# A two-layer kernel in a new order: loads held for the turns of q, and in four batches the normalised product with tokens on partitions

## The chip, the cores and the metric

The kernel runs on one NeuronCore of a Trainium2 chip. The metric is the device time of one execution in microseconds (us), as the median of several runs. The core has a matrix engine (TensorE, "PE" in the profile), VectorE ("DVE"), ScalarE ("ACT"), GpSimd ("POOL") and SyncE ("SP"). Each has one queue of instructions that it works off in order. Transfers run on 16 DMA engines. In this kernel SP issues the stores and the DMA transposes, and POOL issues the loads that also convert float32 to bfloat16.

## What is computed

There are 8 batches of 576 tokens with 8 heads of 64. The first layer is linear attention with a normalisation, the second a channel mix of RWKV's kind:

```
kv  = einsum('bhsd,bhse->bhde', k, v)
u   = einsum('bhsd,bhde->bhse', q, kv)
x   = u / sqrt(mean(u*u, -1) + 1e-6) * g_norm          # heads side by side: [B, S, 512]
xk  = mu_k*x + (1-mu_k)*x_prev ;  xr = mu_r*x + (1-mu_r)*x_prev     # x_prev: the token before
kk  = maximum(xk @ w_k, 0)                             # 512 -> 1024
out = sigmoid(xr @ w_r) * (kk*kk @ w_v)                # 1024 -> 512
```

q, k, v and the output are float32 in HBM.

## The kernel before

The whole program is one list of words, `ORDER`. A loop at the end takes word after word and calls the function of that name, so the list fixes the order of instructions on every engine. A word is a step, its arguments, the PSUM banks that it takes (`=25`), and a `'` where VectorE does the step and not ScalarE. Nothing moves at run time: an engine that waits for one instruction holds all those behind it.

The steps of one batch, with the lines under which the profile knows them:

- `ld.0.b`, `ld.1.b`, `ld.2.b` load k, v and q (POOL; L193 for k and v, L205 and L207 for q's two parts: `in_q`, 512 tokens, and `in_qr`, the other 64). Each of k, v and q has two buffers, so that a load of batch b waits until the batch two before is done with its buffer. Batches 0 and 1 are loaded and worked in pieces by words of their own (`lf`, `kc`, `qc`, `uc`), among matmuls on zeros that bridge waits (`wm`, L246).
- `kv.b` makes kv (PE, L328, 72 matmuls on 64x64 tiles); `kvo` takes it out of PSUM.
- `qd.b.0` turns `in_q` into `qT` by a DMA transpose of 16 blocks (SP, L344); `qd.b.1` turns the small part into `qTr`, 4 blocks (SP, L346).
- `u.b.part` makes u with features on partitions: parts 0 and 1 are 8 matmuls of 256 columns each on 64x64 tiles (PE, L361), part 2 is the small part (L354).
- `sq` squares u (ACT, L372); `ms` makes the mean over a head by a matmul with a matrix of 1/64 (PE, L376; 512 columns in parts 0 and 1); `rs` is the inverse root (ACT, L381); `mu` multiplies u, g and the root into `xT` (DVE, L400).
- `d`, `sc`, `add` make xk and xr (L428, L437/L439, L448). `which` is 0 for xk and 1 for xr.
- `K.b.f.h` is xk @ w_k in 16 pieces of 4 matmuls of 288 columns (PE, L493), `Ko` the maximum with 0 (DVE L457, ACT L455), `ks` the square (DVE L463, ACT L461).
- `R.b.t` is xr @ w_r, 4 matmuls of 512 columns (PE, L513), `S` the sigmoid (ACT, L518); `V.b.t.part` is kk*kk @ w_v, twice 4 matmuls of 512 columns (PE, L523; the last tile in halves, L531); `fin` multiplies (DVE, L538); `st` stores (SP, L555).
- `tab` loads a table of activation functions (ACT, L585).

Steps of several batches stand among each other: `kv.6`, say, stands among the K steps of batch 3.

Of the kernel before, what the change touches and what calls it, by code (L numbers as in the profile page):

```python
# [30 lines left out]
    sc.0.1.2' Kf.0.2.3.256 Kf.6.0.4.256=3 Kf.7.0.4.256=1 Kfo.7.256 Kf.2.3.4.256 Kf.5.0.4.256=4 Kf.0.3.4.256
    Kfo.0.256 Kf.1.2.3.256 Kf.1.3.4.256 sc.0.1.1' add.0.1.0 wm.3=6 qc.1.0.2.0.576=67 qco.1.1.0.576 add.0.1.1
    R.0.2=1 R.0.1=5 R.0.0=7 lf.1.1.2.4.0.576 lw.2.0.0.4.0.4 sc.0.0.2.0.256' Kfo.1.256' sc.0.0.3.0.256' S.0.2
    S.0.1 sc.0.0.1.0.256' add.0.0.0.0.256 qco.1.0.0.576' R.0.3=0 S.0.3 add.0.0.1.0.256 Kfo.2.256' S.0.0
    Kfo.5.256' ksp.0.4.256.576' Kfo.6.256' ksp.4.8.256.576' Kl.0.256=1 lw.2.1.4.8.0.4 ld.2.2 qd.2.0 qd.2.1
    Klo.0.256 kc.1.0.2=65 kco.1.0' tab.0.1 qc.1.2.4.0.576=24 uc.1.0=0 kc.1.2.4=37 kco.1.3 sq.1.0 Kl.1.256=1
    qco.1.2.0.576' kco.1.2' uc.1.4=6 sq.1.4 kco.1.1' qco.1.3.0.576' uc.1.1=2 sq.1.1 uc.1.2=3 Klo.1.256'
    ksp.0.4.0.256' ms.1.0=5 rs.1.0 mu.1.0 Kl.3.256=7 sq.1.2 ms.1.4=4 rs.1.4 mu.1.4 ms.1.1=1 rs.1.1 Klo.3.256'
    Kl.2.256=5 Klo.2.256 ksp.4.8.0.256' ms.1.2=4 uc.1.3=0 sq.1.3 uc.1.5=6 sq.1.5 V.0.2.0=1 rs.1.2 mu.1.1
    ms.1.3=7 rs.1.3 V.0.2.1 ms.1.5=5 rs.1.5 tab.1.1 mu.1.2 V.0.0.0=4 V.0.0.1 mu.1.3 V.0.3.0=2 V.0.3.1 V.0.1.0=7  # L40
    mu.1.5 wrap.1 dc.1.0.2.0.576 sc.1.0.0 dc.1.2.4.0.576 sc.1.0.2 sc.1.0.3' sc.1.0.1' add.1.0.0 add.1.0.1
    sc.1.1.0 sc.1.1.1 V.0.1.1 ld.0.2 ld.1.2 sc.1.1.3 sc.1.1.2' add.1.1.0 add.1.1.1 fin.0.3 K.1.6.0=3 K.1.1.0=5
    Ko.1.1.0 fin.0.2 ld.2.3 K.1.6.1=0 Ko.1.6.0' R.1.8=6 Ko.1.6.1 S.1.8 R.1.4=5 kv.2=02 kvo.2.0 qd.3.1 kvo.2.1
    kvo.2.2' K.1.0.0=1 R.1.7=6 K.1.0.1=3 R.1.6=0 fin.0.1 kvo.2.3 S.1.4 Ko.1.0.0' u.2.1=25 Ko.1.0.1' R.1.5=7
    K.1.5.0=1 fin.0.0 st.0.0 K.1.4.0=3 Ko.1.4.0' S.1.7 S.1.6 sq.2.3 zl K.1.1.1=6 Ko.1.1.1' ks.1.1' Ko.1.5.0'
    K.1.2.0=4 Ko.1.2.0' S.1.5 sq.2.2 ms.2.2=0 tab.0.2 ms.2.3=7 rs.2.3 mu.2.3 K.1.3.0=3 Ko.1.3.0 K.1.7.0=6
    K.1.3.1=1 Ko.1.3.1' rs.2.2 mu.2.2 u.2.2=7 sq.2.4 u.2.0=43 sq.2.1 sq.2.0 ld.0.3 ld.1.3 kv.3=50 ld.2.4 qd.4.1
    Ko.1.7.0' kvo.3.0 ks.1.0' K.1.2.1=1 ks.1.3' Ko.1.2.1 ks.1.2' kvo.3.1 kvo.3.3' K.1.7.1=2 Ko.1.7.1 ks.1.7'
    ms.2.0=6 rs.2.0 mu.2.0 ms.2.1=5 rs.2.1 kvo.3.2 K.1.5.1=1 V.1.4.0=0 K.1.4.1=2 ks.1.6 Ko.1.5.1 ms.2.4=6 rs.2.4
    mu.2.1 d.2.0 d.2.4 d.2.1 V.1.7.0=5 V.1.8.0=4 Ko.1.4.1 ks.1.4' d.2.3 mu.2.4 d.2.2 sc.2.1.0' ks.1.5 tab.1.2  # L50
    V.1.6.0=3 V.1.7.1 V.1.8.1 st.0.3 V.1.4.1 sc.2.0.0 sc.2.0.3 sc.2.0.1' V.1.6.1 qd.3.0 sc.2.1.3' add.2.0.0
    sc.2.0.2' add.2.0.1 sc.2.1.1 add.2.1.0 K.2.5.0=1 sc.2.1.2' K.2.5.1=6 add.2.1.1 K.2.2.1=2 Ko.2.5.0' Ko.2.5.1
    fin.1.4 K.2.2.0=7 Ko.2.2.0' Ko.2.2.1 fin.1.7 ks.2.5' R.2.2=6 S.2.2 fin.1.8 ld.0.4 R.2.3=1 R.2.1=2 S.2.1
    S.2.3 ks.2.2' R.2.0=0 ld.1.4 K.2.3.0=7 Ko.2.3.0' st.0.2 st.1.4 S.2.0 u.3.0=56 sq.3.1 sq.3.0 u.3.2=4 sq.3.4
    K.2.3.1=2 fin.1.6 st.1.6 Ko.2.3.1' K.2.0.0=1 Ko.2.0.0' ks.2.3' ms.3.1=0 K.2.6.0=7 Ko.2.6.0' K.2.4.0=3
    Ko.2.4.0' tab.0.3 K.2.0.1=2 rs.3.1 mu.3.1 ms.3.0=1 ms.3.4=7 K.2.1.0=3 rs.3.4 Ko.2.0.1 ks.2.0' rs.3.0
    K.2.4.1=0 Ko.2.4.1 K.2.1.1=7 K.2.6.1=2 u.3.1=61 Ko.2.1.0' Ko.2.1.1 ks.2.1 kv.4=03 V.2.1.0=7 mu.3.0 sq.3.3
    ms.3.3=5 mu.3.4 sq.3.2 ms.3.2=4 Ko.2.6.1' ks.2.6' rs.3.3 mu.3.3 kvo.4.0 rs.3.2 st.1.7 mu.3.2 V.2.0.0=2 d.3.0
    d.3.4 d.3.1 d.3.2 sc.3.0.0' kvo.4.1 kvo.4.2 tab.1.3 K.2.7.1=5 V.1.5.0=0 K.2.7.0=4 Ko.2.7.0 Ko.2.7.1 V.1.5.1
    V.2.2.0=1 kvo.4.3 ks.2.4 V.2.3.0=3 sc.3.0.1 sc.3.0.3 sc.3.0.2' ks.2.7' V.2.3.1 sc.3.1.0' sc.3.1.1' add.3.1.0  # L60
    ld.2.5 V.2.1.1 V.2.2.1 add.3.0.0 add.3.0.1 K.3.0.0=6 Ko.3.0.0 K.3.0.1=4 K.3.5.0=5 K.3.2.0=6 st.0.1 st.1.8
    qd.4.0 Ko.3.5.0 sc.3.1.3' fin.2.2 sc.3.1.2' K.3.4.0=1 add.3.1.1 R.3.7=5 Ko.3.0.1' ks.3.0' fin.1.5 fin.2.1
    K.3.5.1=4 qd.5.0 fin.2.3 Ko.3.5.1' R.3.8=0 R.3.4=7 S.3.7 st.1.5 qd.5.1 Ko.3.4.0 u.4.1=51 K.3.3.0=3 Ko.3.3.0'
    sq.4.3 S.3.8 sq.4.2 R.3.6=4 S.3.6 R.3.5=3 st.2.2 st.2.3 Ko.3.2.0' K.3.2.1=0 Ko.3.2.1' ks.3.2' K.3.3.1=6
    Ko.3.3.1' V.2.0.1 fin.2.0 S.3.4 S.3.5 K.3.7.0=4 ms.4.3=7 K.3.1.0=3 tab.0.4 rs.4.3 Ko.3.1.0' K.3.1.1=0
    Ko.3.1.1 ms.4.2=6 rs.4.2 ks.3.3 K.3.7.1=2 Ko.3.7.0' ld.0.5 ld.1.5 Ko.3.7.1' kv.5=73 mu.4.2 kvo.5.0' ld.2.6
    kvo.5.1 mu.4.3 u.4.0=40 sq.4.0 ld.0.6 kvo.5.3 ld.1.6 kv.6=62 ld.2.7 ld.0.7 kvo.5.2' sq.4.1 u.4.2=5 sq.4.4
    kvo.6.0' kvo.6.1' ks.3.7' K.3.6.0=3 Ko.3.6.0 K.3.6.1=7 ms.4.1=1 Ko.3.6.1 K.3.4.1=6 ms.4.4=2 ms.4.0=3 ks.3.5'
    ks.3.1' V.3.8.0=7 rs.4.1 kvo.6.3' mu.4.1 rs.4.0 mu.4.0 d.4.0 d.4.1 V.3.7.0=1 d.4.3 Ko.3.4.1 ks.3.4 ks.3.6
    V.3.6.0=3 V.3.8.1 V.3.6.1 rs.4.4 tab.1.4 qd.6.0 mu.4.4 d.4.4 d.4.2 sc.4.1.0 sc.4.1.1' sc.4.1.3 sc.4.1.2  # L70
    fin.3.8 V.3.7.1 add.4.1.0 sc.4.0.0' st.2.1 add.4.1.1 V.3.5.0=0 V.3.5.1 fin.3.6 u.5.0=64 fin.3.7 fin.3.5
    sc.4.0.1 add.4.0.0 st.3.7 st.3.8 u.5.1=25 sq.5.3 sq.5.2 sc.4.0.3' sq.5.1 R.4.3=7 S.4.3 sc.4.0.2' add.4.0.1
    R.4.0=3 S.4.0 R.4.1=1 S.4.1 R.4.2=0 S.4.2 K.4.0.0=7 V.3.4.0=3 ms.5.2=1 Ko.4.0.0 ms.5.3=0 K.4.2.0=7 Ko.4.2.0'
    tab.0.5 rs.5.2 mu.5.2 V.3.4.1 ms.5.1=7 K.4.3.0=1 rs.5.3 K.4.1.0=0 sq.5.0 K.4.0.1=2 mu.5.3 ms.5.0=5 fin.3.4
    rs.5.1 Ko.4.3.0 mu.5.1 Ko.4.1.0' K.4.1.1=7 rs.5.0 mu.5.0 d.5.0 K.4.2.1=1 Ko.4.2.1 Ko.4.0.1 ld.1.7 u.5.2=3
    sq.5.4 kv.7=54 ks.4.2 K.4.5.0=0 Ko.4.5.0 ms.5.4=1 rs.5.4 K.4.3.1=2 Ko.4.3.1 qd.7.1 K.4.4.0=6 st.2.0
    K.4.6.1=0 K.4.6.0=1 ks.4.0' Ko.4.4.0 Ko.4.1.1' ks.4.1 qd.6.1 K.4.7.1=7 d.5.4 mu.5.4 d.5.1 d.5.2 kvo.6.2'
    sc.5.0.0' ks.4.3' Ko.4.6.0' sc.5.1.0' sc.5.0.3 sc.5.0.1' sc.5.0.2 add.5.0.0 add.5.0.1 K.4.4.1=2 kvo.7.0
    V.4.0.0=3 K.4.5.1=6 Ko.4.4.1 K.4.7.0=1 V.4.1.0=5 Ko.4.6.1 Ko.4.5.1' K.5.2.0=2 K.5.6.0=0 ks.4.6 Ko.4.7.0'
    Ko.4.7.1 ks.4.5' kvo.7.1' ks.4.4 ks.4.7' K.5.7.0=7 qd.7.0 Ko.5.6.0' sc.5.1.1' K.5.6.1=6 sc.5.1.3' Ko.5.2.0'  # L80
# [29 lines left out]
def kernel(  # L110
# [536 lines left out]
```

## Time and profile before

| | before |
|---|---|
| median of 3 runs | 210.25 us (209.4 to 211.29) |
| the profiled execution: time, span on the core | 211.27 us, 209.5 us |
| busy: PE, DVE, ACT | 193.4, 147.7, 140.4 us |
| K matmuls (L493) x448 | 64.0 us |
| V matmuls (L523) x280 | 65.4 us |
| R matmuls (L513) x144 | 34.0 us |
| HBM read, written | 33.56 MB, 9.44 MB |
| mean granted clock of PE | 0.976 |

The profile is that of one execution, whose time is beside its span; the span goes from the first instruction to the last and is a little shorter. "PEclk" is the share of full speed that PE's clock was granted. "DMA share" in a table of stretches is busy time of the 16 DMA engines over the stretch; it goes over 1 where packets overlap on an engine.

### The profile page before, as it was taken

The page shows a single profiled execution, that of the slowest core. Times are in us where ns is not written, and L with a number is a line of the kernel's source. Part 1 is how long each engine was busy: PE and PEld are TensorE (multiplying, and loading weights), DVE is VectorE, ACT ScalarE, POOL GpSimd, SP SyncE. Part 2 cuts the span into 40 slices and gives each one's busy share as a digit, 9 for nine tenths or more (in the row PEclk, how much of TensorE's full clock was granted, in tenths as well). Part 3 has the DMA queues.
Part 4 walks back from the last instruction along what each step waited for, and adds up shares of the span by engine and source line. Part 5 has one row for each costly group of instructions (what it writes and reads, how often), then busy time and mean ns, then how long its engine had stood idle before and what let it go on. Part 6 is the DMA issues. An engine that isn't in the chain of part 4 may idle for free.

```text
span 209.5 us, 4772 instructions
## 1 busy us (share of the span) xinstructions
PE 193.4 (92%) x1925; PEld 111.9 (53%) x1925; DVE 147.7 (70%) x331; ACT 140.4 (67%) x263; POOL 31.4 (15%) x49
## 2 busy tenths in 40 slices
PE   7699999995999999999549999999999999999992
PEld 2344565462765576465335457666554576755541
DVE  2159998963699787994617949985499799756242
ACT  2258779953897599638708899926997896625630
POOL 8664242000500500052400000000000000000000
PEclk9889999999999999999958999999999999999999
DMA  6999999999999799999999950732002100024425
GB/s 221 183 195 204 208 206 199 207 179 183 226 203 214 126 189 264 212 106 198 240 159 156 214 179 5 137 126 100 0 3 100 52 0 3 0 79 173 153 63 188
DMA packets 43018, 30.66 MB, mean 146 GB/s; under 512 B 19308, under 2 KB 38004, under 8 KB 42996
## 3 DMA queue, kind: packets, MB, share of 16 engines
q0 software_dynamic: 22672, 16.19, 52.5%
q1 hardware_dynamic: 20164, 14.03, 27.8%
q8 instruction: 15, 0.25, 0.5%
q10 hardware_dynamic: 160, 0.13, 0.2%
q14 instruction: 7, 0.06, 0.1%
HBM read 33.56 MB, written 9.44 MB: 205 GB/s over the span
## 4 chain that ended last, share of the span: by engine, by line
PE 60%; DMA 35%; POOL 1%; issue 1%; DVE 0%; POOLq 0%
PE ps_km L493 22%; PE ps_v L523 22%; DMA qT<-in_q 12%; PE ps_r L513 10%; DMA in_q<-in_q_dram 9%; DMA in_v<-in_v_dram 7%; DMA wk_sb<-in_moe_w_k_dram 4%; DMA q<-in_q_dram 3%; PE ps_ms L376 2%; PE ps_kv L328 1%; PE ps_u L361 1%; PE ps_v L531 1%; PE ps_u L354 1%; POOL in_k L193 0%; POOL wk_sb L214 0%
## 5 line engine op out<-in xcount | busy, mean ns | idle before, releaser
L523 PE MATMUL ps_v<-wv_sb,sqk 128*128 128x512 bf16 x280 | 65.4, 379 | 0.0
L493 PE MATMUL ps_km<-xk,wk_sb 128*128 128x288 bf16 x448 | 64.0, 289 | 0.0
L493 PEld LDWEIGHTS <-wk_sb 128*128 128x128 bf16 x448 | 43.7, 99 | 18.5 <-issue 0.6
L523 PEld LDWEIGHTS <-sqk 128*128 128x128 bf16 x280 | 27.0, 98 | 28.8 <-issue 0.4
L457 DVE TENSOR_SCALAR rt<-ps_km 128x288 bf16<-128x288 f32 (+2 forms) x64 | 28.8, 462 | 19.2 <-PE ps_km L493 18.7
L455 ACT ACTIVATE rt<-ps_km 128x288 bf16<-128x288 f32 (+2 forms) x60 | 23.8, 419 | 21.3 <-PE ps_km L493 21.0
L513 PE MATMUL ps_r<-wr_sb,xr 128*128 128x512 bf16 x144 | 34.0, 379 | 0.0
L538 DVE TENSOR_TENSOR out_sb<-ps_v,sig 128x512 f32<-128x512 f32 (+1 forms) x37 | 24.1, 671 | 11.8 <-PE ps_v L523 6.4
L372 ACT ACTIVATE sq<-ps_u 128x512 bf16<-128x512 f32 (+4 forms) x43 | 21.2, 527 | 15.8 <-PE ps_u L354 5.2
L400 DVE SCALAR_TENSOR_TENSOR xT<-ps_u,cols,rs 128x512 bf16<-128x512 f32 (+4 forms) x43 | 27.3, 659 | 4.2 <-ACT rs L381 4.0
L518 ACT ACTIVATE sig<-ps_r 128x512 bf16<-128x512 f32 x36 | 20.6, 600 | 13.5 <-PE ps_r L513 13.2
L381 ACT ACTIVATE rs<-ps_ms,eps 128x512 f32<-128x512 f32 (+4 forms) x43 | 25.7, 620 | 3.2 <-PE ps_ms L376 3.1
L513 PEld LDWEIGHTS <-xr 128*128 128x128 bf16 x144 | 13.8, 98 | 14.9 <-issue 0.4
L463 DVE TENSOR_TENSOR sqk<-rt 128x576 bf16<-128x576 bf16 (+2 forms) x40 | 18.6, 482 | 2.6 <-ACT rt L455 2.1
L585 ACT ACT_TABLE_LOAD x15 | 19.2, 1283 | 0.3
L437 ACT ACTIVATE m<-dx,cols 128x576 bf16<-128x576 bf16 (+2 forms) x25 | 17.6, 747 | 1.4 <-DVE dx L428 0.8
L461 ACT ACTIVATE sqk<-rt 128x576 bf16<-128x576 bf16 x20 | 13.4, 680 | 1.2 <-DVE rt L457 1.1
L376 PE MATMUL ps_ms<-sq,means 128*128 128x512 bf16 (+4 forms) x43 | 13.5, 349 | 0.6 <-ACT sq L372 0.4
L439 DVE TENSOR_SCALAR m<-dx,cols 128x576 bf16<-128x576 bf16 (+2 forms) x41 | 13.7, 362 | 0.2
L205 POOL DMA_DIRECT2D in_q<-in_q_dram x6 | 5.3, 891 | 49.5 <-DMA qT<-in_q 48.3
L448 DVE TENSOR_TENSOR xr<-m,xT 128x1152 bf16<-128x1152 bf16 x16 | 11.9, 754 | 0.6 <-ACT m L437 0.3
L448 DVE TENSOR_TENSOR xk<-m,xT 128x1152 bf16<-128x1152 bf16 (+2 forms) x17 | 11.6, 699 | 0.7 <-ACT m L437 0.3
(66 smaller groups left out, 131.5 us busy)
## 6 DMA issues: line engine op xcount, KB each, us to landing
out_dram<-out_sb SPq DMA_DIRECT2D x23, 256.0 KB, 2.9
in_k<-in_k_dram POOLq DMA_DIRECT2D x7, 576.0 KB, 15.2
in_v<-in_v_dram POOLq DMA_DIRECT2D x6, 576.0 KB, 16.2
in_q<-in_q_dram POOLq DMA_DIRECT2D x6, 512.0 KB, 12.9
out_dram<-out_sb SPq DMA_DIRECT2D x24, 128.0 KB, 6.8
wk_sb<-in_moe_w_k_dram POOLq DMA_DIRECT2D x4, 256.0 KB, 8.8
wv_sb<-in_moe_w_v_dram POOLq DMA_DIRECT2D x2, 512.0 KB, 16.7
sqk<-in_k_dram SPq DMA_DIRECT2D x1, 576.0 KB, 3.7
```

Source lines behind the costliest of these rows:

```text
L372: ACT.activation(out=sq[:, :ps.shape[1]], in_=ps, func=AF.Square)
L381: ACT.activation(out=rs[:, :ps.shape[1]], in_=ps, func=AF.Abs_reciprocal_sqrt, bias=eps)
L400: DVE.scalar_tensor_tensor(out=dst, in0=ps, scalar=g_sb, in1=rs, op0=ALU.mult, op1=ALU.mult)
L448: DVE.tensor_add(out=blended(a, which)[:, hs, c0:c1], in0=at[a]["m", which][:, hs, c0:c1], in1=xT[a % 2][:, hs, P + c0:P + c1])
L455: eng.activation(out=dst, in_=ps, func=AF.Relu)
L457: eng.tensor_scalar(out=dst, in0=ps, scalar1=0.0, scalar2=None, op0=ALU.max)
L493: nc.tensor.matmul(ps, wk_sb[:, cc, 128 * fc:128 * fc + 128], at[b]["xk"][:, cc, SH * h:SH * h + SH], start=(cc == 0), stop=(cc == NHP - 1))
L513: nc.tensor.matmul(ps, xr[:, cc, 128 * t:128 * t + 128], wr_sb[:, cc, :], start=(cc == 0), stop=(cc == NHP - 1))
L518: ACT.activation(out=sig[b, t], in_=give(("r", b, t)), func=AF.Sigmoid)
L523: nc.tensor.matmul(ps, sqk[:, fc, 128 * t:128 * t + 128], wv_sb[:, fc, :], start=(fc == 0), stop=(fc == NFC - 1))
L538: DVE.tensor_mul(out=o, in0=give(("v",) + key), in1=sig[b, t][:, c])
L585: "tab": lambda eng, n, b: ACT.preload_act_table_set(("abs_reciprocal_sqrt_and_small", "sigmoid_and_others")[n]),
```

## The change

**The order.** Every step stands at a new place. All 8 batches are still computed, with the same tiles for K, R and V.

**Loads and q's turns.** A new word `gt.b` is a copy of one column from `qTr` on POOL. POOL can't go on to its next load before the small turn of q of batch b has landed. It stands behind the loads of batch 2 (`gt.2`), behind those of batch 3 (`gt.3`), and, for batches 4, 5 and 6, behind the last load of all. In batch 2 the small turn now goes ahead of the large one, as it did in batch 3. In these lines the loads that followed one another on POOL are:

```
before: q2 k2 v2 q3 k3 v3 q4 k4 v4 q5 k5 v5 q6 k6 v6 q7 k7 v7
after:  q2 k2 v2 gt.2 q3 v3 k3 gt.3 v4 k4 q4 q5 v6 v5 k6 q6 k5 v7 q7 k7 gt.4 gt.5 gt.6
```

**The last four batches.** In batches 4 to 7 the parts 0 and 1 of `u` are made with tokens on partitions and heads and features along the row: `ut`, 16 matmuls of 64 columns each with a stationary piece of 64 x 128 of `qT`. `sqt` squares (ACT), `rdt` sums 64 neighbours (DVE), `rst` is the inverse root on 128x16 (ACT), `mut` multiplies (DVE) into a tile `y`, which has 3 buffers, `yd` turns `y` into `xT` by a DMA transpose of 4 blocks (SP), and `gs` multiplies by g (DVE). The mean by matmul (`ms`), `rs` and `mu` are left for the small part alone in these batches.

**Counts of the two programs** where they differ most: PE matmuls of `ms` on 512 columns 28 and 12; `u` on 256 columns 96 and 32; `ut` 0 and 128; matmuls on zeros 31 and 19. DVE: `mu` on 512 columns in batches 2 to 7 24 and 8; `rdt` 0 and 16; `mut` 0 and 16; `gs` 0 and 8; `Ko` on 288 columns 57 and 52; `sc` 37 and 32; `ks` 36 and 31. ACT: `rs` on 512 columns 28 and 12; `rst` 0 and 8; `Ko` 55 and 60; `sc` 23 and 28; `ks` 20 and 25. SP: 16 more DMA transposes.

```
+    gates = const.tile([128, B], BF16, name="gates")
...
+    def gate(a):
+        POOL.tensor_copy(out=gates[:, a:a + 1], in_=at[a]["qTr"][:, 0, 0:1])
...
+    def u_t(a, tp):
+        ps = [take(("t", a, 2 * tp + r), [128, H, HD], FP32, "ps_u") for r in range(2)]
+        for h in range(H):
+            for r in range(2):
+                nc.tensor.matmul(ps[r][:, h, :], at[a]["qT"][half(r), 2 * h + tp, :], kv_on(a, h // 2, h % 2, r), start=True, stop=True)
+
+    def square_t(a, t):
+        sq = at[a]["sqt", t] = work.tile([128, 512], BF16, tag="sq", name="sq", bufs=SQ_BUFS)
+        ACT.activation(out=sq, in_=held["t", a, t].rearrange("p h d -> p (h d)"), func=AF.Square)
+
+    def sum_t(a, t):
+        ss = mine(a, "ss", [128, 4, H], FP32)
+        DVE.tensor_reduce(out=ss[:, t, :], in_=at[a]["sqt", t].rearrange("p (h d) -> p h d", h=H), op=ALU.add, axis=AX.X)
+
+    def rsqrt_t(a, tp):
+        ACT.activation(out=mine(a, "rst", [128, 4, H], FP32)[:, 2 * tp:2 * tp + 2, :], in_=at[a]["ss"][:, 2 * tp:2 * tp + 2, :],
+                       func=AF.Abs_reciprocal_sqrt, scale=1.0 / HD, bias=eps)
+
+    def mult_t(a, t):
+        y = at[a]["y", t] = work.tile([128, 512], BF16, tag="y", name="y", bufs=SQ_BUFS)
+        DVE.tensor_mul(out=y.rearrange("p (h d) -> p h d", h=H), in0=give(("t", a, t)),
+                       in1=at[a]["rst"][:, t, :].unsqueeze(2).to_broadcast([128, H, HD]))
+
+    def y_turn(a, t):
+        c = place(a)[0] + 256 * (t % 2) + 128 * (t // 2)
+        nc.sync.dma_start_transpose(out=xT[a % 2][:, :, c:c + 128], in_=at[a]["y", t])
+
+    def gain(a, r):
+        x = xT[a % 2][:, :, place(a)[0] + 256 * r:place(a)[0] + 256 * r + 256]
+        DVE.tensor_scalar(out=x, in0=x, scalar1=g_sb, scalar2=None, op0=ALU.mult)
```

Two pieces of the new `ORDER` that the prediction speaks of, the first around the first `ut`, the second around `kv.5`:

```
ms.3.3=3 ld.1.5 ld.0.6 rs.3.3 V.1.6.0=5 zl mu.3.3 V.1.6.1 qd.4.1 st.0.1 K.2.6.0=1 u.3.2=2
fin.1.6 kvo.4.2 ut.4.0=03 ks.2.0 st.1.4 sq.3.4 ms.3.4=7 ks.2.5' mu.3.2 d.3.0 ld.2.6 ks.2.3 V.2.0.0=5
...
st.1.7 S.3.8 sqt.4.1 st.2.0 sc.3.0.3' R.3.4=2 fin.2.2 S.3.4 S.3.6 sqt.4.0 qd.5.0 ...
rst.4.0 K.3.2.0=2 Ko.3.2.0' K.3.1.0=7 Ko.3.1.0 ut.4.1=56 sqt.4.2 sqt.4.3 u.4.2=4 sq.4.4 kv.5=12 kvo.5.0
kvo.5.1 mut.4.1 K.3.7.0=7 Ko.3.7.0 yd.4.1 mut.4.0 yd.4.0 rdt.4.2 rdt.4.3 K.3.3.1=3 K.3.0.1=0 Ko.3.0.1
K.3.1.1=1 Ko.3.1.1 rst.4.1 mut.4.2 ms.4.4=2 mut.4.3 rs.4.4 st.2.2 ...
```

In the order before, `kv.5` and `kv.6` stand at:

```
Ko.3.1.1 ks.3.3 K.3.7.1=2 Ko.3.7.0' ld.0.5 ld.1.5 Ko.3.7.1' kv.5=73 mu.4.2 kvo.5.0' ld.2.6
kvo.5.1 mu.4.3 u.4.0=40 sq.4.0 ld.0.6 kvo.5.3 ld.1.6 kv.6=62 ...
```

## The prediction

> **What bounds the kernel now.** I read the page first: PE is busy 92% of the span, so time goes by PE's work and by the places where PE stands still.
>
> ```profile
> PE 193.4 (92%) x1925; PEld 111.9 (53%) x1925; DVE 147.7 (70%) x331; ACT 140.4 (67%) x263; POOL 31.4 (15%) x49
> ```
>
> The waits of PE name those places. After the start there are two, both for a DMA: the first u of batch 2 for its turned q, and kv of batch 6 for v.
>
> ```profile
> PE ps_kv L328 <- DMA in_v<-in_v_dram: 5.4, 1, 5.4
> PE ps_u L361 <- DMA qT<-in_q: 2.6, 1, 2.6
> ```
>
> The chain of waits shows how they come about: a turn of q lasts 14.1 us in one place; the next q's load is held by another turn, and v6 queues behind that load on POOL.
>
> ```profile
> 37.39 14.10 DMA qT<-in_q
> ...
> 80.43 10.48 DMA qT<-in_q
> ...
> 93.75 13.87 DMA in_v<-in_v_dram
> 107.61 0.14 issue
> 107.75 1.18 PE ps_kv L328 x55
> ...
> 109.14 2.04 PE ps_km L493 x8
> ```
>
> A turn's price depends on the loads beside it, as the rows of the tile qT show (issue to landing: shortest, median, longest). The shortest ran when the loads were over. The waits of POOL show the other side: loads held for turns.
>
> ```profile
> DMA to landing us min/median/max: 4.3/5.6/14.1
> ...
> POOL in_q L205 <- DMA qT<-in_q: 48.3, 3, 18.3
> ```
>
> In the table of stretches (PE, PEld, DVE, ACT, POOL busy, then clock, DMA share, GB/s) the wait for v6 also halves the clock. The stretch of 115 to 190 us shows PE full without a gap and DVE at 80%, ACT at 74%.
>
> ```profile
> 50.00:55.00 5.00, 3.47 (x30) 2.29 (x31) 1.03 (x4) 2.63 (x4) 1.95 (x3) 1.00 1.22 200
> 70.00:75.00 5.00, 5.00 (x44) 2.89 (x42) 3.88 (x9) 3.51 (x7) 3.08 (x4) 1.00 0.76 111
> 90.00:95.00 5.00, 5.00 (x39) 2.81 (x37) 3.79 (x8) 1.32 (x4) 3.56 (x5) 1.00 0.72 115
> 105.00:110.00 5.00, 2.25 (x84) 1.88 (x85) 0.82 (x4) 0.38 (x1) 0.00 (x0) 0.50 1.43 157
> 115.00:190.00 75.00, 75.00 (x582) 44.44 (x581) 60.07 (x131) 55.77 (x103) 0.00 (x0) 1.00 0.28 77
> ```
>
> **PE's work.** Rates come from the dense pieces of the chain: 4 K matmuls 0.49 us, 4 V or R 0.86, one 512-column mean 0.216, 16 matmuls of u (two parts) 0.56 to 0.68, one kv 0.61. Batches 4 to 7 lose 8 parts of u, 8 x 0.3 = 2.4, and 16 means, 16 x 0.216 = 3.5: -5.9. They gain 8 `ut` of 16 loads and 16 matmuls. No row has a 64x128 load before a 64-column matmul. From below: the small part of u, 8 in 0.12, 0.015 each, gives 8 x 0.24 = 1.9. From above: the weight load's row, 98 ns, one after another, 8 x 1.57 = 12.5. The nearest is kv, 72 pairs of load and matmul in 0.61: four tiles at a time, so 34 ns for a pair with 64 columns to load. Twice the columns and two tiles at a time (the two halves of qT) make about 54 ns for a load, half of it each: 0.43 per `ut`, 3.4 in all. Net -2.5 (bounds -4.0 and +6.6). Of the 12 fewer matmuls on zeros, 9 stood in the first 19 us, where PE waits for data; they are worth nothing. Three stood in dense work at 23.3 us: 3 x 0.216 = -0.65.
>
> The Trainium skill, page "TensorE: Matmul & The Clock Gate", section "LDWEIGHTS (loading the stationary operand)", puts a load at columns / 1.2 ns, 107 ns for 128, and has loads overlap only across row groups; by that a `ut` would be 0.85 and the net about +1. The kv row is faster than that rule: 53 ns for 64 columns would not fit into 34.
>
> **The two old waits.** The order of loads and the gates take away their causes: v and k of batch 4 no longer stand behind q, v6 stands ahead of q6, and the small turn of q2 goes first, with nothing but k2 and v2 beside it. I take off 2.6 and 5.35, and 2.0 for the half clock (8 K matmuls took 2.04 and not 0.98; the rest of kv, u and the mean some 0.9). Sum -9.9.
>
> **The new waits for DMA.** Where are they? I count PE's work up to a step by the rates above (matmuls on zeros left out) and set it against the clock. Before, the first u of batch 2 stands behind 32.3 us of work and was reached at 49.0: 16.7 later. POOL's loads up to v2 are the same transfers in the same order, and the start is paced by them, so I keep 16.7 (give or take 1.5 for the other order of the start). After, without waits, u of batch 2 is due at 52.7, kv.3 at 57.5, u.3 at 67.8, `ut.4.0` at 79.5, kv.5 at 92.1, kv.6 at 98.7.
>
> Against that the transfers. q2 lands at 37.4 and v2 near 44, as before. The small turn (2.3 us at the fastest, 10.0 at the slowest) opens `gt.2` near 43; qT of batch 2 lands near 48, in time for 52.7. q3 lands near 50 (a load issued on an idle queue took 6.6 to 8.3), k3 near 57: kv.3 just in time. `gt.3` opens near 55; then v4, k4, q4 land near 61, 65, 69. SP issues the large turn of batch 3 behind six stores, near 56: 66 to 71, so u.3 waits 0 to 3. The turn of batch 4 starts at 69 to 70 with q5, v6, v5 and k6 under way and no gate before these: 10.5 to 14.1 us, so 80 to 84, against 79.5. The wait here is about 4 us. PE works in order, so everything shifts with it.
>
> kv.5 needs k5, the ninth load behind k3. Before, the nine loads behind v3 (landed 56.7) ended at 107.6, 51 us, with two breaks at the shares of 0.76 and 0.72, some 5 us. Without breaks that is 46 us from 57: 103. By the faster rates between (2.8 to 3.5 us for a k or v, 3.1 to 5 for a q) I come to 97. I take 100, 8 us behind 92.1; the 4 of the turn are part of it. Then kv.6 and the rest have their data. Bounds: 0, if loads keep their best pace and the turn ends early; 14, if k5 lands at 103 and a turn of q5 behind it costs 3 more. Value 8.
>
> The 16 turns of y have 4 blocks like the small q turn: 2.3 us free, up to 10.0 beside loads. SP issues the first two right behind qT of batch 5, whose issue alone took up to 6.9 us, near 99. y has three buffers, so the fourth `mut` of batch 4 holds DVE until the first turn has landed, and behind it wait the `Ko` that free PE's banks. PE has 3 to 4 us of matmuls until a bank is missing: I take +1 (0 to 4). The later turns run after the loads, with 20 us between `ut` and K to hide them.
>
> **VectorE.** In batches 4 to 7 it loses 16 `mu` (0.746): -11.9. It gains 16 sums, 16 `mut` and 8 `gs`. `mut` is like the final product, 512 columns from PSUM, 0.685; `gs` on 1024 bf16 lies between 0.364 (576 columns) and 0.692 (a subtraction of 1024), I take 0.45. No reduction stands in the trace: 0.417 (bf16 subtraction on 512) and 0.746 are the bounds, 0.685 my value. Together 22.0 + 3.6 = 25.6, less 11.9, less 6.3 for five `Ko`, `sc` and `ks` each that go to ScalarE: +7.4. Over the 75 us of that stretch 60.1 becomes 67.5 of about 72.5: 93%. ScalarE loses 16 `rs` (11.0), gains 8 `rst` (0.3, near the 0.374 of its 128-column form) and 9.3 of moved work: +0.7. Both still fit under PE's work, at nothing; if that cover were gone, DVE's 7.4 would count in full.
>
> The Trainium skill, page "VectorE: DVE Perf Modes", section "The perf-mode tier table", has a reduction at one element per cycle whatever the type and its rules call it the slowest operation of this engine. No run here shows it so far; at 0.417 the sum for DVE would be +3.1 and not +7.4.
>
> **The end.** Before, the last product is half a tile (0.42) and the store 64 KB; now a whole tile (0.685) and 256 KB: +0.4.
>
> **Sum** on the profiled execution: -2.5 - 0.65 - 9.9 + 8 + 1 + 0.4 = -3.7. The span goes from 209.5 to 205.8, its time from 211.27 to 207.6. That execution is 1.0 above the median, so the median goes to 206.5.
>
> **The rivals.**
> 1. *The gates do all that they are for.* POOL's loads end early enough and qT of batch 4 lands before 79.5: the 9 us of new waits go, 197.5. For it: POOL issues as soon as it can, and both breaks of the share are loads that come too late. Against it: no gate stands before the loads beside the turn of batch 4.
> 2. *VectorE becomes the bound in the last four batches.* At 93% there are 5 us to spare in the 75. It decides from there on: when the pairs of a sum and a `mut` take 0.3 us more than I have (16 x 0.3 = 5), or when the hand-overs between ACT and DVE (square, sum, root, product) and the turns of y hold DVE's queue for as long. At 12 us lost, 0.75 for each of 16 tiles, PE waits 7 us more: 213.5. For it: the work between K of batch 6 and K of batch 7 asks DVE for some 10 us beside 10.7 of PE. Against it: before, DVE ran through such stretches (60 to 65 us, 4.89 of 5) without a wait of PE.
> 3. *Weight loads bound `ut`.* At 98 ns, two at a time, a `ut` takes 0.78: +2.8, 209.3, no change. The rule of columns / 1.2 named above is this case. Against it: the kv row.
>
> **Chances.** Forecast 0.45, rival 1 0.18, rival 2 0.27, rival 3 0.10. A measurement of this kernel can tell about 1% from no change, so faster means below 208.1, slower above 212.4. The forecast's own range (203 to 210) is faster in 0.37 and the same in 0.08; rival 1 is faster; rival 2 is slower in 0.21 and the same in 0.05; rival 3 is the same in 0.04, faster in 0.03, slower in 0.03. Faster 0.59, same 0.17, slower 0.24. The range is 199.5 to 213.5: it takes in most of rival 1 and 2 and the bounds of the new waits; `ut` at its upper bound (+9) is left out.
>
> **What would show it.** PE's waits: right if none stands at u of batch 2 and kv.6, and some 4 to 8 us in all at `ut.4.0` or kv.5 for DMA; wrong if there is none (rival 1), or if PE waits for DVE in batches 4 to 7 (rival 2). The `ut` row: 0.43 each. The reduction's row: near 0.685. The page's DVE total: near 152. Of the whole the forecast is wrong if the median is above 208.

## The result, and the profile after

The changed kernel takes 217.1 us (median of 4 runs, 215.3 to 217.5) against 210.7 (209.4 to 211.3). The ratio is 1.030, with an interval of 1.022 to 1.037: slower, where the prediction said 206.5. Of some kernels a few executions took over 1.5% longer than the fastest: ratios leave these out where enough others are left, medians hold them, so the two can differ a little.

The profiled execution took 216.82 us with a span of 215.1. The busy line of its page, in the order of the one shown of before:

```profile
PE 191.9 (89%) x1961; PEld 111.5 (52%) x1961; DVE 153.2 (71%) x334; ACT 141.9 (66%) x276; POOL 32.7 (15%) x54
```

PE's busy time fell by 1.5 us while the span grew by 5.6, so PE stands still for longer. The waits of PE after (engine, line, what it waited for, sum, times, longest):

```profile
PE ps_u L375 <- DMA qT<-in_q: 7.9, 1, 7.9
PE ps_km L531 <- DVE y L391: 3.2, 1, 3.2
PE ps_kv L330 <- DMA in_k<-in_k_dram: 2.4, 1, 2.4
...
PE ps_v L561 <- DVE kv L243: 0.9, 1, 0.9
```

The two old waits (u of batch 2, kv of batch 6) are gone. There are four new ones: `kv.3` for k3, the first `ut` of batch 4 for its turned q, and two where PE waits for VectorE, which itself is held. The chain of waits after shows by what:

```profile
38.44 6.32 DMA qTr<-in_qr
44.76 0.05 issue
44.81 0.19 POOL gates L351
...
47.35 11.01 DMA in_k<-in_k_dram
...
58.40 0.78 PE ps_kv L330 x72
...
74.33 16.20 DMA qT<-in_q
90.53 0.05 issue
90.58 0.61 PE ps_u L375 x16
...
108.06 0.70 DVE y L391
...
109.87 8.66 DMA xT<-y
118.53 0.03 issue
118.55 0.48 DVE xT L400
```

`gt.2` opens at 44.8 and only then q3, v3 and k3 are issued; k3 lands at 58.4. q of batch 4 lands at 74.3 and its turn takes 16.2 us, up to 90.5, while PE stood at `ut.4.0` from 82.65. In batch 4 the product `y` (L391) and the step by g (L400) hang on the turns of y. The rows of the tile y, with who waited (us, times) and then issue to landing (shortest, median, longest):

```profile
  DVE y L391: 6.1, 3
  PE ps_km L531: 3.2, 1
  DVE xT L400: 1.9, 1
...
DMA to landing us min/median/max: 2.4/3.2/8.7
```

The longest of these are the turns issued from 105.6 on, the last of them landed at 118.5, beside the loads of v7 and q7 and a store; the shortest come later, with no load beside them. The rows of POOL and PE in that stretch (start, us, what, in brackets the idle time before it) show v7 issued right behind the end of `kv.5`, and PE standing still:

```profile
105.58 0.74 POOL L195 DMA_DIRECT2D in_v<-in_v_dram  x1 [12.17 <-PE ps_kv L330]
...
114.12 1.12 PE L531 MATMUL ps_km<-xk,wk_sb 128*128 128x288 bf16 x4 [3.20 <-DVE y L391]
```

Over the same stretches as before, and some more, the table (PE, PEld, DVE, ACT, POOL, clock, DMA share, GB/s) shows where the clock goes:

```profile
55.00:60.00 5.00, 2.57 (x88) 1.38 (x87) 4.29 (x8) 2.33 (x5) 1.43 (x3) 0.94 1.13 262
...
85.00:90.00 5.00, 0.00 (x0) 0.00 (x0) 0.00 (x0) 0.00 (x0) 0.00 (x0) 0.67 1.30 126
90.00:95.00 5.00, 4.42 (x29) 2.08 (x30) 2.75 (x8) 2.59 (x5) 2.32 (x3) 0.64 1.02 239
...
110.00:115.00 5.00, 1.80 (x12) 0.99 (x9) 1.59 (x4) 1.48 (x4) 0.00 (x0) 0.90 1.33 185
115.00:120.00 5.00, 4.07 (x113) 2.69 (x113) 3.08 (x10) 3.48 (x8) 0.00 (x0) 0.75 1.25 230
120.00:205.00 85.00, 85.00 (x660) 50.54 (x659) 72.64 (x154) 59.01 (x112) 2.42 (x5) 1.00 0.41 97
```

At 85 to 90 us every engine is idle and only transfers run. From 120 us on PE has no gap. All that was lost was lost before.

**The account of 5.6 us of span.** Gaps of PE over 0.1 us after 20 us of the span: 8.1 before, 14.8 after. Matmul time at half clock after 20 us: 3.5 before (104.5 to 111.3), and after 3.4 (59.4 to 62.8), 3.0 (86.7 to 93.6) and 3.3 (114.0 to 117.5), 9.7 in all; half of it is lost, 1.8 and 4.9. The tail behind the last matmul grew by 0.2. So +6.7 + 3.1 + 0.2 = +10.0. The span grew by 5.6, so PE's work and the start together gave 4.4; this is the remainder, not a measurement. By place: `kv.3` 2.4 + 1.7, `ut.4.0` 7.9 + 1.5, the hold by the y turns 3.2 + 0.9 + 1.7.

The rows of the new operations (busy us, mean ns of one):

```profile
L391 DVE TENSOR_TENSOR y<-ps_u,rst 128x512 bf16<-128x512 f32 x16 | 10.7, 687 | 8.1 <-DMA xT<-y 6.1 <-ACT rst L386 1.9
L383 DVE TENSOR_REDUCE ss<-sq 128x8 f32<-128x512 bf16 x16 | 10.4, 678 | 1.1 <-ACT sq L379 1.1
L400 DVE TENSOR_SCALAR xT<-xT,cols 128x1024 bf16<-128x1024 bf16 x8 | 3.8, 479 | 1.9 <-DMA xT<-y 1.9
L375 PE MATMUL ps_u<-kv,qT 64*128 64x64 bf16 x128 | 3.6, 208 | 7.9 <-DMA qT<-in_q 7.9
L375 PEld LDWEIGHTS <-qT 64*128 64x128 bf16 x128 | 2.8, 106 | 8.9 <-DMA qT<-in_q 8.0 <-issue 0.7
```

### The profile page after: what moved, and what is told of

Same layout as the page of the kernel before. It is cut to its first block, busy times and chain, and to the rows that moved or that the text cites. A ratio compares the mean times of both kernels' runs of the same rounds, so it can differ in the third digit from the quotient of the medians.

```text
span 215.1 us, 4891 instructions
## 1 busy us (share of the span) xinstructions
PE 191.9 (89%) x1961; PEld 111.5 (52%) x1961; DVE 153.2 (71%) x334; ACT 141.9 (66%) x276; POOL 32.7 (15%) x54
## 4 chain that ended last, share of the span: by engine, by line
PE 58%; DMA 36%; POOL 2%; DVE 1%; issue 1%; SPq 0%; ACT 0%; POOLq 0%
PE ps_v L561 25%; PE ps_km L531 18%; PE ps_r L551 11%; DMA in_qr<-in_q_dram 8%; DMA qT<-in_q 8%; DMA wr_sb<-in_moe_w_r_dram 5%; DMA in_k<-in_k_dram 5%; DMA xT<-y 4%; DMA q<-in_q_dram 3%; DMA qTr<-in_qr 3%; PE ps_kv L330 1%; PE ps_u L375 1%; PE ps_v L569 1%; POOL wk_sb L216 1%; PE ps_ms L414 1%
## 5 line engine op out<-in xcount | busy, mean ns | idle before, releaser
L531 PE MATMUL ps_km<-xk,wk_sb 128*128 128x288 bf16 x448 | 59.0, 287 | 3.2 <-DVE y L391 3.2
L576 DVE TENSOR_TENSOR out_sb<-ps_v,sig 128x512 f32<-128x512 f32 (+1 forms) x37 | 24.0, 671 | 10.4 <-issue 4.1
L495 DVE TENSOR_SCALAR rt<-ps_km 128x288 bf16<-128x288 f32 (+2 forms) x57 | 25.0, 465 | 8.8 <-PE ps_km L531 8.4
L438 DVE SCALAR_TENSOR_TENSOR xT<-ps_u,cols,rs 128x512 bf16<-128x512 f32 (+4 forms) x27 | 16.0, 608 | 14.7 <-ACT rs L419 14.4
L475 ACT ACTIVATE m<-dx,cols 128x576 bf16<-128x576 bf16 (+1 forms) x29 | 20.9, 759 | 8.2 <-DVE dx L463 3.5
L419 ACT ACTIVATE rs<-ps_ms,eps 128x512 f32<-128x512 f32 (+4 forms) x27 | 15.2, 581 | 13.1 <-PE ps_ms L414 12.8
L499 ACT ACTIVATE sqk<-rt 128x576 bf16<-128x576 bf16 x25 | 16.6, 680 | 3.5 <-DVE rt L495 3.1
L501 DVE TENSOR_TENSOR sqk<-rt 128x576 bf16<-128x576 bf16 (+2 forms) x35 | 16.5, 487 | 0.9 <-ACT rt L493 0.6
L391 DVE TENSOR_TENSOR y<-ps_u,rst 128x512 bf16<-128x512 f32 x16 | 10.7, 687 | 8.1 <-DMA xT<-y 6.1
L410 ACT ACTIVATE sq<-ps_u 128x512 bf16<-128x512 f32 (+4 forms) x27 | 12.6, 487 | 5.2 <-PE ps_u L359 4.2
L383 DVE TENSOR_REDUCE ss<-sq 128x8 f32<-128x512 bf16 x16 | 10.4, 678 | 1.1 <-ACT sq L379 1.1
```

The lines of the kernel that those rows point to most:

```text
L475: eng.activation(out=out_, in_=in_, func=AF.Copy, scale=mu)
L495: eng.tensor_scalar(out=dst, in0=ps, scalar1=0.0, scalar2=None, op0=ALU.max)
L499: eng.activation(out=dst, in_=src, func=AF.Square)
L501: eng.tensor_mul(out=dst, in0=src, in1=src)
L531: nc.tensor.matmul(ps, wk_sb[:, cc, 128 * fc:128 * fc + 128], at[b]["xk"][:, cc, SH * h:SH * h + SH], start=(cc == 0), stop=(cc == NHP - 1))
L576: DVE.tensor_mul(out=o, in0=give(("v",) + key), in1=sig[b, t][:, c])
```

## The experiments

The explanations go by letters. A (runs 1 to 4): the gates hold the loads longer than the faster turns give back, and y's three buffers hold VectorE. B (runs 2 and 4): the new form asks too much of VectorE. C (from run 5 on): what the DMA engines have to move in the first 105 us is given; the new order asks for its data some 5 to 8 us too early, and an edit of order moves the wait and does not remove it. D, the rival of C in run 5: a turn is slow because it shares the engines with loads, and nothing else counts. Words of `ORDER` are shown as the edit where that is all. Lines of the experiments are a few lower than those of the changed kernel, since their list is wrapped otherwise (`ut` is L370 and `u` L361, in place of L375 and L366). "Before" ran beside each group: 210.5 to 211.0.

**1. No gates.**

```
- every gt.2 gt.3 gt.4 gt.5 gt.6
```

> The changed kernel without any gate (the words gt.2 to gt.6 are left out), else the same. Theory A, the gates cost more than they give: they kept POOL from loading for 16.4 and 10 us while the DMA engines ran out of loads, so q3 landed at 51.3 and q4 at 74.3. Without them q3 lands near 48.5, k3 near 56.7 (wait of kv.3 2.4 to under 1), q4 near 68, the large turn of batch 4 ends near 82 to 84 and not at 90.5, so that its wait falls from 7.9 to 0 to 4 us, with less half clock: 208 to 212 us. Rival, the gates protect the turns: the first u of batch 2 waits for its turn again (2 to 5 us), the turn of batch 4 still takes 16 us or more, and the time stays at 216 us or rises.

Measured 219.2 (215.0 to 221.0), ratio 1.027 (1.016 to 1.038). The waits of PE:

```profile
PE ps_u L361 <- DMA qT<-in_q: 7.3, 1, 7.3
...
PE ps_kv L325 <- DMA in_k<-in_k_dram: 5.1, 1, 5.1
```

The wait at `ut.4.0` is gone, and 7.3 us stand at u of batch 2 and 5.1 at `kv.5`. A falls: the gates move the wait.

**2. Six buffers for y; 3. both edits.**

```
-        y = ... tag="y", name="y", bufs=SQ_BUFS)
+        y = ... tag="y", name="y", bufs=6)
```

> The changed kernel with 6 buffers for y and not 3. Theory A, the turns of y cost only through y's buffers: the wait of the product (L391) for DMA xT<-y, 6.1 us, goes, and with it PE's 3.2 and 0.9 us around 111 to 119 us and the half clock behind them (1.7): 211 to 213.5 us. Rival B, the new form of u asks too much of VectorE: the same delay shows as waits of PE for other DVE work, 216 us or more.

> Both edits together: no gates, 6 buffers for y. Theory A: the two gains add, 203 to 208 us, faster than the kernel before; PE waits 0 to 4 us after its start. Rival (gates protect the turns, or VectorE is the bound): 212 us or more.

Measured 218.8, ratio 1.039 (1.032 to 1.046), and 219.4, ratio 1.032 (1.025 to 1.040). With six buffers `mut` no longer waits, but the step by g does, and PE behind it:

```profile
DVE xT L395 <- DMA xT<-y: 6.9, 1, 6.9
...
PE ps_v L556 <- DVE kv L238: 6.1, 1, 6.1
```

So the buffers alone are not the cause; VectorE waits for the late turns all the same. Without gates as well, most of it stands at `kv.5` (10.2 for k5).

**4. The new order with the old form of u** in batches 4 to 7 (`sq`, `ms`, `rs`, `mu` in the places of the new steps, no y, six buffers for the squares).

> The new order with its gates, but batches 4 to 7 make u in the old form (features on partitions, mean by matmul, root on 512 columns, one product into xT; no turn of y, no g step); 6 buffers for squares and roots. This leaves the order's DMA waits and takes away the new form. Theory A, the form costs only through y's buffers: PE has 3.2 us more to do (8 parts of u and 16 means against 8 ut), the wait of 7.9 us stays, the hold by y goes: 213 to 217 us, about 3 us slower than the kernel with 6 buffers for y. Rival B, the form's VectorE work and hand-overs cost time by themselves: faster than that kernel, 208 to 211 us.

Measured 231.1, ratio 1.096 (1.087 to 1.106). PE's gaps grow to 21.9 us, 6.8 of them in seven waits for ScalarE's roots, and its busy time to 197.1, while 6.7 at u of batch 4 remain. This order is laid out for the new form, so both forecasts missed, and the run does not tell A and B apart.

**5. Less to transfer:** the stores of batches 0 and 1 left out, these rows are not written.

```
         o = outs.pop(key)
+        if b < 2:
+            return
```

> The changed kernel without the stores of batches 0 and 1 (those rows of the output stay unwritten): 2.4 MB less for the DMA engines before 100 us, all else the same. Theory C, the first 105 us are bound by what the DMA engines move (loads, turns and stores together) and the order asks for its data 5 to 8 us before it can be there: PE's waits for DMA up to kv.5, 10.4 us in all, fall by 4 to 8, and the time to 208 to 213 us. Rival D, what counts is only that a turn shares the engines with loads in flight, whatever else there is: the wait at the first ut stays at 6 to 8 us and the time at 215 us or more.

Measured 213.0, ratio 1.013 (1.009 to 1.017): 4.1 below the changed kernel, 3.6 by the ratios. The wait at `ut.4.0` shrinks from 7.9 to 5.0 and the hold from 4.1 to 2.7. The amount to move matters, but is not all.

**6. The later loads held for the y turns.** A copy from `xT` on POOL (`gy.4`) behind the last y turn of batch 4, so that v7, q7 and k7 are issued after it; the turn of q5 goes ahead of one store.

```
+    def hold_y(a):
+        c = place(a)[0] + 256 + 128
+        POOL.tensor_copy(out=gates[:, a - 4:a - 3], in_=xT[a % 2][:, 0, c:c + 1])
...
- st.2.0 ... qd.5.0 ... yd.4.3
+ qd.5.0 st.2.0 ...     yd.4.3 gy.4
```

> The changed kernel with one more gate on POOL, ahead of the loads of v7, q7 and k7, that opens when the last turn of y of batch 4 has landed; and the large turn of batch 5 issued ahead of the store before it (st.2.0), so that it does not stand in front of the turns of y. Theory C: the turns of y then take 3 to 5 us each and not 8 to 9, VectorE's holds (6.1 us at the product, 1.9 at the g step) and PE's 4.1 us behind them shrink to under 1, the half clock there goes: 211 to 214 us. Rival: the hold comes from the hand-overs themselves, PE still waits 3 us or more around 110 to 120 us and the time stays at 216 us or more.

The gap at 110 us is gone from the profile: the y turns of batch 4 land 3.0 to 3.6 us after their issue, where the first three of the changed kernel took 7.6 to 8.7. That execution took 213.3, 3.5 below the one of the changed kernel, of which 2.6 are a shorter wait at `ut.4.0` (5.3) that this edit does not aim at; three others took 216.6 to 218.8. The spread is wider than the effect, so this run shows where the hold comes from and not what it is worth (ratio 1.029, 1.019 to 1.040).

**7. No `gt.3`, and k5 ahead of q6** (loads q5 v5 k5 v6 k6 q6).

> The changed kernel without the gate of batch 3 and with v5, k5 ahead of v6, k6 (and q6 behind them) in POOL's order. Theory C: v4, k4 and q4 land some 6 us earlier, the turn of batch 4 ends near 83, the wait at the first ut falls from 7.9 to 0 to 3 us, and kv.5 no longer stands behind v6, k6, q6: waits for DMA before 100 us of 2 to 5 us in all, 209 to 213 us. Rival D: the turn beside loads takes 16 us or more wherever it stands, some wait of 6 us or more stays, 215 us or more.

Measured 214.0, ratio 1.013 (1.004 to 1.023). No wait is left at `ut.4.0` or `kv.5`; 4.4 us stand at u of batch 3, for its turn, and 2.3 + 2.5 at the hold by the y turns.

**8. The kernel before with q6 behind k6 and v6,** the new order's cure for the old wait at `kv.6`.

```
- ... ld.2.6 ... ld.0.6 ... ld.1.6 ...
+ ...            ld.0.6 ... ld.1.6 ld.2.6 ...
```

> The kernel before with one word moved: the load of q6 behind those of k6 and v6. POOL then doesn't hold k6 and v6 for the turn of batch 4. Theory C: v6 lands near 95 to 100 and not at 107.6, kv.6 waits 0 to 1 us and not 5.4, the half clock behind it goes: 203 to 206 us, faster than the kernel before. Rival, the DMA engines are the bound there too: v6 lands hardly earlier or another transfer is late in its place, and the time stays within 1% of 210.5 us.

The runs lie between 212.7 and 218.2, without a ratio, above the 210.5 of before. In the profile (of an execution of 217.35) the wait at `kv.6` is gone, and the turn of q of batch 4 takes 22.1 us with k6 and v6 issued right behind it, so that u of batch 4 waits 7.3. As in the new order, loads that no longer wait run beside a turn.

**9. As 7, with the turn of q3 ahead of the six stores of batch 0 on SP; 10. the same with 6.** E: SP's queue alone made the wait at u of batch 3.

```
- qd.3.1 ... st.0.0 ... st.0.3 st.0.2 ... qd.3.0
+ qd.3.1 ... qd.3.0 st.0.0 ... st.0.3 st.0.2 ...
```

> As the version without gt.3 and with k5 ahead of q6 (214.0, one wait of 4.4 us at u of batch 3), but the large turn of q3 stands on SP ahead of the six stores of batch 0, so that SP issues it some 5 us earlier. Theory C (what the DMA engines move in the first 105 us, asked for 5 to 8 us too early, sets the sum of the waits): the wait at u of batch 3 shrinks to 1 to 3 us, but the first ut of batch 4 or kv.5 then waits 2 to 4 us more; 212.5 to 214.5. Theory E (SP's queue order alone made that wait): the wait goes and none takes its place; 209 to 211.

> As the run with the early turn of q3, and in addition the later loads (v7, q7, k7) are held on POOL until the y turns of batch 4 have landed, and the turn of q5 stands ahead of st.2.0 on SP. Theory that the hold of VectorE by the y turns is a cost of its own (some 4 us of idle and half clock): the gaps of PE at 108 to 120 us go, 208 to 210.5, level with the kernel before. Theory C in its strict form (a wait removed in one place comes back in the next): a wait at u of batch 6 or kv.7 of 2 to 4 us, 211.5 to 214.

Measured 217.4, ratio 1.038 (1.030 to 1.045), and 214.0, ratio 1.013 (1.006 to 1.019). The wait at u of batch 3 shrinks from 4.4 to 1.6 (and 1.5 more for `fin`, whose buffers wait for the late stores), and the hold by the y turns grows from 4.8 to 8.8; with the loads held it is 4.0. PE comes earlier to a place where the transfers are not done, as C says. E falls, and so does the hope of 208 to 210.5 for run 10.

**11. A gate for batch 4 ahead of q5,** so that no load is issued behind its turn.

```
+ qd.4.0 qd.4.1 gt.4 ld.2.5 ...
```

> The changed kernel with the gate of batch 4 (and both turns of its q) ahead of the load of q5, so that the turn of q4 runs with no load issued behind it. Theory D (the turn is slow only because it shares the engines with q5, v6, v5 and k6): the turn takes 6 to 9 us and not 16.2, the first ut of batch 4 waits 0 to 1.5 us, and nothing else is later: 210 to 213. Theory C: the loads behind it land 6 to 9 us later, kv.5 waits 5 to 9 us for k5, the sum of the waits stays: 215 to 220.

Measured 219.2, ratio 1.045 (1.036 to 1.053). `ut.4.0` does not wait, and kv.5 does:

```profile
PE ps_kv L325 <- DMA in_k<-in_k_dram: 15.9, 3, 13.6
```

The large turn of q of batch 4, issued with no load behind it, landed after 4.4 us and not 16.2: D is right about what makes a turn slow. The sum of the waits did not shrink: there C is right.

**12. Run 10 without the stores of batches 0 and 1** (rows not written).

> As the run with both edits (early turn of q3, k5 first, no gt.3, loads held for the y turns), and the stores of batches 0 and 1 are left out, so these rows are not written. It shows what the new order costs when the DMA engines have less to do in the first 105 us. Theory C: no wait of more than 1.5 us is left after the start and PE ends 3 to 5 us earlier than with the stores: 205 to 207, some 4 us below before, which is what the fewer instructions on PE (3.2) and the two old waits with their half clock (9.7, less what is left) allow. If VectorE or PE's own work is the bound, the stores change nothing: within 1 us of the run with the stores.

Measured 210.8, ratio 1.005 (1.000 to 1.009): 3.2 below run 10 by the medians and 1.7 by the ratios, which hardly clears their intervals. The forecast of 205 to 207 missed: `kv.7` waits 3.0, with 3.0 lost to the half clock. VectorE is held there by a y turn of batch 5 (8.7 us, from 119.0), which now runs beside the loads that had been held for those of batch 4.

**13 to 15. The two turns taken away by themselves.** H: the hold by the y turns of batch 4 is a price of its own. T: so is the wait for the large turn of q of batch 4. Without `yd.4.*` 512 tokens go on with older values in `xT`; without `qd.4.0` VectorE writes zeros where the turned q would be.

```
- yd.4.1 ... yd.4.0 ... yd.4.2 ... yd.4.3     (13, 15)
...
+        if part == 0 and a == 4:              (14, 15)
+            DVE.memset(mine(a, "qT", [128, 16, 128], BF16), 0.0)
+        elif part == 0:
```

> The changed kernel without the four y turns of batch 4, so that 512 tokens of that batch go on with older values of xT. Nothing can then hold VectorE at mut in batch 4. Theory H (the hold is a price of its own): the gaps of 3.2 and 0.9 us at 110 and 118 us and the 1.7 us that the half clock behind them costs go, 5.8 of 216.8 in all: 210 to 212. Theory C in its strict form (a wait that is removed comes back in the next place): u or kv of batch 6 or 7 waits instead, 215 to 217.

> The changed kernel without the large turn of q of batch 4: VectorE writes zeros into that tile in its place (one instruction, below 1 us), so the 512 tokens are those of a q of zeros. The load of q6 no longer waits for that turn. Theory T (the wait at the first ut is the turn's alone): the 7.9 us and 1.5 us of half clock go and nothing takes their place, 207 to 208.5. Theory C: PE comes to kv.5 at 96.5 and finds k5 missing for 0 to 4 us, and the y turns of batch 4, now started some 8 us earlier beside loads, hold VectorE for 4 to 7 us: 210 to 214.

> Both of these edits together. Both waits are then gone with what made them: T and H give 216.8 - 9.4 - 5.8 = 201.6; theory C leaves 0 to 4 us at kv.5 and 0 to 3 at the data of batch 6 or 7: 203 to 208.

| left out | median us | ratio to before |
|---|---|---|
| nothing (the changed kernel) | 217.1 | 1.030 (1.022 to 1.037) |
| y turns of batch 4 | 211.1 | 1.001 (0.998 to 1.005) |
| large turn of q of batch 4 | 211.7 | 1.003 (0.998 to 1.008) |
| both | 203.4 | 0.964 (0.959 to 0.970) |

The hold costs 6.0, as 3.2 + 0.9 + 1.7 = 5.8 of the profile said: H holds. The turn of q costs 5.4 (5.7 by the ratios) and not its 9.4. In run 14 the y turns start earlier, beside the loads, and the waits (of all engines; the profiled execution took 212.76) show what comes back:

```profile
DVE xT L397 <- DMA xT<-y: 7.2, 1, 7.2
PE ps_v L558 <- DVE kv L238: 6.5, 1, 6.5
...
PE ps_kv L325 <- DMA in_k<-in_k_dram: 5.2, 2, 3.4
```

So T falls, and a part of the wait comes back as C says. With both turns gone the kernel is 13.7 us faster than the changed kernel, and 7 us faster than before. That is 2.3 more than 6.0 + 5.4, no more than the intervals of the ratios leave open, so it is not shown that the two waits stand in for each other. Of PE's waits after 35 us in the profile of run 15 (an execution of 206.16) only those for k are longer than 0.15 us:

```profile
PE ps_kv L325 <- DMA in_k<-in_k_dram: 4.6, 3, 2.3
```

So the engines can do the work in 203.4 or less when these two transfers cost nothing.

**16. Run 7 with the loads held as in 6; 17. the same with six buffers for y; 18. run 10 with six buffers.**

> No gt.3 and k5 ahead of q6 (214.0 by itself, with 4.4 us at u of batch 3 and 4.8 us in two gaps of the y hold), with v7, q7 and k7 held until the y turns of batch 4 have landed and the turn of q5 ahead of st.2.0. Unlike the run with the early turn of q3, SP's order at batch 3 is as in the changed kernel. Theory H: the 4.8 us and some 1.7 of half clock go, 208 to 210. Theory C strict: the y turns still begin beside loads (q6 is late here), 2 to 4 us of hold stay: 211 to 214.

> The version with no gt.3, k5 first and the later loads held for the y turns (211.7: waits of 4.1 at u of batch 3 and 2.4 at the y hold, 1.6 of half clock behind that), with six buffers for y. With three buffers the fourth mut waits for the first turn and the fourth turn is issued at 108.6; with six all four are issued by 106 and no load is beside them. Theory H with the loads held: the hold goes and does not come back at the g step, 207 to 209, below the kernel before. Rival (as with six buffers alone, where the wait moved to the g step, 6.9 us on VectorE): the g step waits as long as mut did, 211 to 213.

> The same with the turn of q3 ahead of the six stores of batch 0 on SP (214.0 with three buffers of y: 1.9 + 1.4 at batch 3, 4.0 at the y hold, 2.5 of half clock behind it). If six buffers take the hold away, the earlier turn gives its 1 us as well: 206.5 to 208.5. If the y turns are slow because of q6 and the stores beside them, and not for want of buffers, the wait goes to the g step: 213 to 216.

| run | median us | ratio to before |
|---|---|---|
| 16 | 211.7 | 1.004 (1.000 to 1.008) |
| 17 | 210.4 | 0.999 (0.995 to 1.002) |
| 18 | 213.6 | 1.013 (1.009 to 1.016) |

The waits of run 17:

```profile
DVE xT L399 <- DMA xT<-y: 3.2, 1, 3.2
...
PE ps_kv L325 <- DMA in_k<-in_k_dram: 2.5, 1, 2.5
...
PE ps_v L560 <- DVE kv L238: 2.4, 1, 2.4
...
PE ps_u L361 <- DMA qT<-in_q: 2.3, 1, 2.3
```

Order and buffers give back the 6.4 us that the change lost, and no more: 17 is level with before. The hold went to the step by g once more, as the rival of its expectation said, though at half the size of run 2. The loads were held, but the first y turns still took 6.5 to 7.5 us, beside the load of q6, which landed at 107.1. The forecast of 207 to 209 missed. 16 and 17 against 10 and 18 differ in the turn of q3 alone: issuing it ahead of the stores costs 1.8 and 2.9 us by the ratios, the first hardly clear of their intervals.

## Why the prediction was wrong

**Right: the work.** `ut` took 0.34 us, two of them 0.68 in the chain, and not 0.43, so u and the means gave 3.2 and not 2.5.

```profile
161.47 0.68 PE ps_u L375 x32
```

VectorE's rows are 678, 687 and 479 ns against 685, 685 and 450. Its total is 153.2; the text's "near 152" does not follow from its own +7.4, which makes 155.1. The Trainium skill's rule that a reduction runs at one element per cycle whatever the type ("VectorE: DVE Perf Modes", "The perf-mode tier table") agrees for bf16, the one type here: 678 ns for 512 elements, as long as a product from PSUM of that width. Run 15, at 203.4, shows that the engines can do the work in less time than before.

**Right: the old waits.** Both are gone, 7.9 us and 1.8 of clock, 9.7 against 9.9.

**Wrong: the term of the new waits, +8 and +1.** They came to 14.5 us of idle time and 4.9 of half clock, 19.4 for 9. Three things were too small.
- *The half clock behind the new waits was put at nothing,* although the same text took off 2.0 for the half clock behind an old one. That is 4.9 us.
- *The waits for DMA, 8, came to 10.4.* `kv.3`, "just in time", waited 2.4: PE came 1.5 us early (55.97 for 57.5) and k3 1.4 late. The other 7.9 look like the 8, but by luck: the text had some 4 at `ut.4.0` and as much at `kv.5`, and all of it stood at `ut.4.0`. `gt.3` opened at 58.2 and not 55, since the small turn of q3, issued at 51.7, took 6.5 us; three loads later q4 landed at 74.3 and not 69. Then the turn took 16.2, above the 10.5 to 14.1 of the rows of before, with four loads in flight beside it (run 11 had 4.4 without them). Together they put the end at 90.5 instead of 80 to 84. `kv.5` waited no more, since PE came late (k5 landed at 101.2, forecast 100).
- *The y turns.* The mechanism was named (three buffers, the fourth `mut`, the K evictions behind it), its size was not: 4.1 us of PE instead of 1, beside 1.7 of the half clock above. They got the price of one small turn, without the question what starts at the same moment: `kv.5` stands right there in the order, its end frees v7's buffer, and q7 stands behind v7. These loads were issued at 105.6 and 106.3, with the first two y turns (105.6 and 107.2).

**The rivals.** That the gates do all (197.5) falls by the profile, with four new waits where it had none. Weight loads do not bound `ut`: their row has 106 ns each, but 16 of them lie in 0.34 us. By the Trainium skill, "TensorE: Matmul & The Clock Gate", a load takes columns / 1.2 ns ("LDWEIGHTS (loading the stationary operand)") and overlaps with matmuls only across row groups ("The mechanism"); the estimate from both is 0.85 for the 16, so the first agrees and the sum does not. VectorE is not the bound by its work: from 120 to 205 us it is busy 85% of the time (forecast 93%) and PE has no gap. But the sign named for that rival, PE waiting for DVE in batch 4, appeared: VectorE was held by a transfer, not busy (1.59 of 5 us at 110 to 115).

What the order of the turns costs beyond batch 4 was not taken apart, nor what an order laid out for it would give with the old form (run 4).

## What to carry to other kernels

Where transfers set the pace, price a new order by the latest landing that each step needs, and look at what a delay there starts next to it: cures at one place (no gates, more buffers, an earlier turn) brought the wait back at the next. Book the half clock for a new wait as for one that goes away. To learn what a wait is worth, take its cause away alone and then with its neighbour: 6.0, 5.4 and 13.7 us told more than any of the reorderings.

## What the runs showed of the hardware

**The half clock goes by a fixed grid.** The periods at half clock begin and end on a grid of 3.413 us that lies differently in each execution. On that grid, in the profiles of before, after and all experiments and after 20 us, all 38 windows at full clock in which PE was idle for 1.94 us or more were followed by one at half clock; of some 980 with up to 1.87 us of idle time one was (1.66). A window at half clock was followed by another in every case with 0.75 us or more of idle time, and by full clock with 0.70 or less. So the wait of 2.56 us before cost no clock (it was split, 0.9 and 1.7, over two windows), and that of 2.43 after did. The Trainium skill, "TensorE: Matmul & The Clock Gate", "What's actually happening", has the free-running window of 3413 ns, which agrees, but speaks of an idle window of that length; here some 57% of one was enough.

**A turn's price depends on what runs beside it.** The large turn of q of batch 4 took 4.4 us in run 11 with no load issued behind it, 16.2 beside four loads, and 22.1 in run 8; the y turns of 128 KB took 2.4 with no load in flight, 3.0 to 3.6 in run 6 and up to 8.7 beside two loads and another turn.
